# Lower halves of weights subtracted on GpSimd in operations of 128 columns, and later weight blocks cut four steps apart

## The chip, the cores and the metric

The kernel runs on one core of a Trainium2 chip. Its engines work side by side, each through its own queue of instructions: TensorE (PE, with its weight loads as PEld), VectorE (DVE), ScalarE (ACT), GpSimd (POOL) and SyncE (SP), which here issues the DMA transfers. They wait for one another by semaphores. The metric is the device time of one execution in microseconds (us), as the median of several runs.

## The reference

A block with attention and a gated feed-forward part, on x of 2048 rows and 512 columns, in float32:

```
xn  = layernorm(x)                                  # over the 512 columns
q, k, v = split(xn @ wqkv)                          # 32 heads of 16
p   = softmax(mask(q k^T / 4))                      # a row sees itself and the 255 before it
s   = (p v) @ wo
g   = silu( (silu(xn @ w1) * (xn @ w3)) @ w2 )      # 512 -> 1792 -> 512
out = x + s * g
```

## The kernel before

**Numbers.** PE multiplies float16. So that the result has float32 accuracy, every operand is a pair: the upper part `hi` is the value rounded to float16, and the lower part `lo` is what the rounding left, also float16. A product takes three matmuls (hi by hi, lo by hi, hi by lo). A weight must first be brought to the middle of float16's range: the sums of squares of its columns or rows are taken (`squares`, L249 on ACT and L251 on DVE), a tiny matmul spreads them over the partitions, and a chain of DVE operations on one to four columns (`powers`, L294 to L304) makes a power of two of them. Only then can the weight be cut in two.

**Cutting a weight.** A raw weight tile has 128 partitions and 512 columns in float32. `split_pool` cuts it in three steps: ACT multiplies the raw tile by its power of two in place (L342), ACT casts it to float16 (L343), and POOL subtracts the cast from the scaled tile (through `halves`, whose line is L339), in two operations of 256 columns. The 28 tiles of w1 and w3 (two for each of 14 blocks f of the 1792), the ten tiles of w2 with f = 4 to 13 and the four of wo go through it. The first four tiles of w2 and the weights of q, k and v go through `split`, which subtracts on DVE. `halves` serves other work too, above all the cutting of the hidden blocks (`rest` in `gate_up`, behind the cast L1068) and of the attention's output.

**Where PE uses it.** In `gate_up` (matmuls on L1035) PE takes a weight tile in four chunks of 128 columns, for each the upper part, the lower part and the upper part again. In the first quarter of the rows (t = 0) the cut weight is also stored to DRAM, from which the later quarters load it.

**Stages.** The 2048 rows are worked through in four quarters of 512. Attention is made in units (a quarter, a group of eight heads, a half of that), and the feed-forward work is laid between their steps. Weights are measured and cut in the first 175 us or so, during the first quarter, except wo. In the same time the rows of the next quarter are normalised (`rstd`, L464 to L473 on POOL, and `centre`, L476 on DVE), the masks are added (L752, DVE) and the maxima are taken (L678, DVE) and negated (L690 and L691, DVE) and the exponentials taken (L755, ACT). The product of gate and up is finished by L1054 and L1059 on DVE and L1050 on ACT. `measure_down` measures w2: squares on ACT (L922), then small DVE operations (L934 to L944) up to the factor `sw` that scales its tiles on ACT (L342).

**What sets the order.** PE's order is the order in which the program writes its matmuls. It is written in steps: `later(n, f)` puts f in a list to be run n steps on, and `step()`, called after each piece of matmul work, runs what is due. The other engines' orders are made by the tile layer, which places instructions by their dependencies and by when they were written. Tiles lie in 54 buffers (`take`, `give`); `give(..., after=5)` offers a buffer again five steps later, and `take` picks the one that has been free the longest, so that a change of steps also changes which tile lies where.

**Around the change.** `measure(f)` handles two blocks f and f+1, four tiles. Its inner `rest` makes the scales and puts four `cut`s in the list, which the diff touches; `cut` takes a float16 buffer, calls `split_pool` and gives the raw tile back.

Of the kernel before, what the change touches and what calls it, by code (L numbers as in the profile page):

```python
# [21 lines left out]
P = 128  # L22
# [61 lines left out]
def tile_block(ctx: ExitStack, tc: tile.TileContext, x, wqkv, wo, w1, w3, w2, out):  # L84
    nc = tc.nc
# [27 lines left out]
    def take(dtype):  # L113
        free.sort()
        slot = free.pop(0)[2]
        made = fpool.tile([P, 512 if dtype == F32 else 1024], dtype, name=slot, tag=slot, bufs=1)
        held[id(made)] = slot, made
        return made

    def give(*tiles, after=0):  # L120

        for made in tiles:
            given[0] += 1
            free.append((now[0] + after, given[0], held.pop(id(made))[0]))
# [19 lines left out]
    def later(n, f):  # L144
        made_so_far[0] += 1
        queue.append((now[0] + n, made_so_far[0], f))
# [35 lines left out]
    def beside_scores(n, f):  # L182

        later(n, lambda: besides.insert(0, f))
# [55 lines left out]
    def squares(parts, on_act=0, apart=0):  # L240


        ssq = small.tile([P, len(parts)], F32, name="ssq")

        def one(i, raw):

            sq = ppool.tile([P, D], BF16, name="sqa" if i < on_act else "junk", bufs=1)
            if i < on_act:
                nc.scalar.activation(sq, raw, AF.Square, accum_out=ssq[:, i:i + 1])  # L249
            else:  # L250
                nc.vector.tensor_tensor_reduce(out=sq, in0=raw, in1=raw, scale=1.0, scalar=0.0,  # L251
                                               op0=ALU.mult, op1=ALU.add, accum_out=ssq[:, i:i + 1])
        for i, raw in enumerate(parts):
            if apart:
                later(apart * (i + 1), lambda i=i, raw=raw: one(i, raw))
            else:
                one(i, raw)
        sb = small.tile([P, len(parts)], BF16, name="sb")

        def cast():  # L260
            lasts["cast"] = nc.vector.tensor_copy(sb, ssq)
        def behind_bank():

            with tc.issue_after(lasts["emptied"].ins) if "emptied" in lasts else nullcontext():
                cast()
        if apart:
            later(apart * (len(parts) + 1) + 1, behind_bank)
        else:
            cast()
        return sb  # L270

    def powers(sb, n, p2, inv, s=None):


        m = sb.shape[-1] // n
        al = small.tile([P, n], F32, name="al")
        if s is None:
            ps = scores_bank()[:, 0, 0:n]
            for i in range(m):
                nc.tensor.matmul(ps, onesb, sb[:, i * n:(i + 1) * n], start=i == 0, stop=i == m - 1)  # L280
        else:
            for h in range(2):
                for c in range(2):
                    for i in range(m):
                        nc.tensor.matmul(s[64 * c:64 * c + 64, h, WIN:WIN + n],
                                         onesb[64 * h:64 * h + 64, 64 * c:64 * c + 64],
                                         sb[64 * h:64 * h + 64, i * n:(i + 1) * n], start=i == 0, stop=i == m - 1)

        def rest():
            if s is None:  # L290
                nc.vector.tensor_scalar(al, ps, 2.08, 1e-30, op0=ALU.mult, op1=ALU.max)
            else:
                with urgent():
                    nc.vector.tensor_scalar(al, s[:, 0, WIN:WIN + n], 2.08, 1e-30, op0=ALU.mult, op1=ALU.max)  # L294
                    nc.vector.scalar_tensor_tensor(al, s[:, 1, WIN:WIN + n], 2.08, al, op0=ALU.mult, op1=ALU.add)

        def chain():
            nc.vector.tensor_scalar(al.bitcast(I32), al.bitcast(I32), 24, 23, op0=ALU.logical_shift_right,
                                    op1=ALU.logical_shift_left)
            if inv is not None:  # L300

                lasts["scale"] = nc.vector.tensor_scalar(inv.bitcast(I32), al.bitcast(I32), -1.0,
                                                         (2 * 127 - 63 + WS_EXP) * 2.0**23, op0=ALU.mult, op1=ALU.add)
            nc.vector.tensor_scalar(p2, al, 2.0**63, None, op0=ALU.mult)  # L304
        return rest, chain

    def then(s, read, *made):

        first, *rest = *(read if isinstance(read, tuple) else (read,)), *made

        def chain():
            for f in rest:
                f()

        def behind_bank():
            with tc.issue_after(lasts["emptied"].ins) if "emptied" in lasts else nullcontext():
                chain()

        def now_and_later():
            first()  # L320
            later(2, behind_bank)
        if s is not None:
            return now_and_later
        first()
        chain()
# [10 lines left out]
    def halves(op, out, a, b):  # L336

        for c in (slice(0, 256), slice(256, 512)):
            op(out[:, c], a[:, c], b[:, c])  # L339

    def split_pool(hi, lo, raw, s):
        nc.scalar.activation(raw, raw, AF.Copy, scale=s)  # L342
        nc.scalar.copy(hi, raw)  # L343
        halves(nc.gpsimd.tensor_sub, lo, raw, hi)


    WQ = {}
# [524 lines left out]
    def measure(f, apart=0):  # L872

        raws = [RAW.pop(f + i) for i in range(2)]
        sb = squares([raws[0][0], raws[1][0], raws[0][1], raws[1][1]], on_act=4 if f > 2 else 2, apart=apart)

        def scale(s=None):
            pp = small.tile([P, 2, 2], F32, name="pp")
            pi = small.tile([P, 2, 2], F32, name="pi")
            return then(s, powers(sb, 4, pp.rearrange("p a b -> p (a b)"), pi.rearrange("p a b -> p (a b)"), s),  # L880
                        lambda: rest(pp, pi))

        def rest(pp, pi):
            ff = slice(f, f + 2)
            nc.vector.tensor_scalar(sg_scale[:, ff], pp[:, 0, :], 0.5 / (WS * XS), None, op0=ALU.mult)
            nc.vector.tensor_mul(p13[:, ff], pp[:, 0, :], pp[:, 1, :])
            measured.update((f, f + 1))

            def cut(i, k):
                if k == 0:  # L890
                    WF[0, f + i] = [[None, None], WF.pop((0, f + i), [None, None])[1]]
                WF[0, f + i][0][k] = a = take(F16)
                split_pool(a[:, 0:D], a[:, D:], raws[i][k], pi[:, k, i:i + 1])
                give(raws[i][k], after=5)
            for i in range(2):
                for k in range(2):
                    later((1, 2, 4, 6)[2 * i + k], lambda i=i, k=k: cut(i, k))
        if started:
            beside_scores(8, scale)
        else:  # L900
            later(10 if apart else 6, scale)
# [12 lines left out]
    def measure_down(k, f):  # L914
# [17 lines left out]
        def rest(p2):  # L932
            assert measured >= set(range(f0, f1))
            nc.vector.tensor_mul(p2, p2, p13[:, f0:f1])  # L934
            q = small.tile([P, 1], F32, name="q")
            nc.vector.tensor_reduce(q, p2, axis=AX.X, op=ALU.max)
            nc.vector.tensor_scalar(down_scale[:, k:k + 1], q, 1.0 / (HS * WS), None, op0=ALU.mult)
            if k:
                nc.vector.tensor_max(fold_q, fold_q, q)
            else:  # L940
                nc.vector.tensor_copy(fold_q, q)
            nc.vector.reciprocal(q, q)
            sw = small.tile([P, 4], F32, name="sw2")
            nc.vector.tensor_scalar(sw[:, 0:n], p13[:, f0:f1], q, WS, op0=ALU.mult, op1=ALU.mult)  # L944

            def cut(f):
                raw = RAW2.pop(f)
                WF.setdefault((0, f), [[None, None], None])[1] = b = take(F16)
                if k == 0:
                    with tc.issue_after(lasts["emptied"].ins):  # L950
                        split(b[:, 0:D], b[:, D:], raw, sw[:, f - f0:f - f0 + 1])
                else:
                    split_pool(b[:, 0:D], b[:, D:], raw, sw[:, f - f0:f - f0 + 1])
                give(raw, after=5)
            for i, f in enumerate(range(f0, f1)):
                later(1 + 2 * i, lambda f=f: cut(f))
            if f1 == FB:
                later(4, fold_scales)
# [663 lines left out]
    for n, u in enumerate(units):  # L1622
# [17 lines left out]
        k = n // 2 + 2  # L1640
# [35 lines left out]
```

## Time and profile before

| | before |
|---|---|
| median of 3 runs | 813.12 us (813.05 to 813.95) |
| profiled execution | 813.03 us |
| its span | 811.2 us, granted clock 1.000 |
| PE busy | 794.5 us, 98% |
| DVE busy | 634.2 us, 78% |
| ACT busy | 392.5 us, 48% |
| POOL busy | 364.0 us, 45%, 648 instructions |

The span runs from the first to the last instruction of the profiled execution; the rest of its time lies around it. A row of a timeline gives the start and the duration in us, the engine, the line, the operation, output and inputs with shapes, how many instructions the row stands for, and in square brackets how long the engine stood idle before it and what ended that. A row of a group gives the busy time and, behind it, the mean duration of one in ns. A row on a line of the source gives the least, the middle and the greatest duration in ns.

### The profile page before, as it was taken

To read this page: it belongs to the slowest core of one execution; us is meant where nothing else is said; L and a number is where in the kernel's file an instruction comes from. 1 tells how busy PE (TensorE), PEld (TensorE's weight loads), DVE (VectorE), ACT (ScalarE), POOL (GpSimd) and SP (SyncE) were. 2 spreads that over 40 slices of the span, in tenths; PEclk is the share of its full clock that TensorE was granted. 3 is DMA by queue.
4 is the path that set the end of the run, shared out by engine and by line. 5 is a ranking of instruction groups with operands and counts; after the bars stand their busy time and mean duration, and the time that the engine had idled before them with its cause. 6 is when DMAs were issued, how large, how long until landed. Compare 5 with 4: busy or idle time off the path is not lost.

```text
span 811.2 us, 23867 instructions
## 1 busy us (share of the span) xinstructions
PE 794.5 (98%) x9176; PEld 404.2 (50%) x9176; DVE 634.2 (78%) x2037; ACT 392.5 (48%) x591; POOL 364.0 (45%) x648
## 2 busy tenths in 40 slices
PE   8999989999999999999999999999999999999998
PEld 4444444444544444444444454456544654466465
DVE  8788788887898777887988888777777887875437
ACT  6879586563536554445444434344444234344421
POOL 2234266232329546354354355530246277560670
PEclk9999999999999999999999999999999999999999
DMA  9978554835566375657655634656462544335321
GB/s 283 253 221 264 156 190 124 283 117 190 158 180 215 127 249 140 214 145 251 171 162 175 193 98 132 174 150 176 116 189 72 162 138 139 113 85 174 112 67 60
DMA packets 109794, 134.18 MB, mean 165 GB/s; under 512 B 18864, under 2 KB 64880, under 8 KB 109680
## 3 DMA queue, kind: packets, MB, share of 16 engines
q1 hardware_dynamic: 109392, 132.13, 54.7%
q8 instruction: 72, 1.18, 0.6%
q10 hardware_dynamic: 288, 0.52, 0.2%
q14 instruction: 42, 0.34, 0.1%
HBM read 91.23 MB, written 36.57 MB: 158 GB/s over the span
## 4 chain that ended last, share of the span: by engine, by line
PE 80%; DVE 9%; ACT 5%; issue 3%; DMA 2%; SPq 0%; DVEq 0%; POOL 0%; ACTq 0%
PE m L1035 30%; PE po L773 8%; PE m L1260 8%; PE m L1178 8%; PE m L596 7%; PE s L745 5%; PE m L1312 4%; PE m L566 4%; PE s L664 3%; DVE junk L678 2%; PE po L664 2%; ACT sqa L249 1%; ACT slot L342 1%; ACT pt L755 1%; DMA dW<-slot 1%
## 5 line engine op out<-in xcount | busy, mean ns | idle before, releaser
L1035 PE MATMUL m<-XH,slot 128*128 128x512 f16 x896 | 267.3, 380 | 1.6 <-DVE slot L617 1.2
L755 ACT ACTIVATE pt<-s,es 128x1024 f32<-128x1024 f32 x152 | 167.7, 1113 | 192.8 <-DVE s L752 174.6
L339 POOL TENSOR_TENSOR slot<-slot,slot 128x256 f16<-128x256 f32 (+1 forms) x170 | 113.2, 694 | 212.2 <-ACT slot L1068 85.0
L1035 PEld LDWEIGHTS <-slot 128*128 128x128 f16 x1344 | 124.8, 98 | 155.9 <-issue 12.4
L1035 PE MATMUL m<-XL,slot 128*128 128x512 f16 x448 | 169.8, 379 | 0.0
L752 DVE TENSOR_TENSOR s<-s,MK 128x256 f32<-128x256 f32 (+2 forms) x280 | 118.8, 435 | 50.7 <-PE s L745 46.4
L678 DVE CUSTOM_DVE_ANT_0 junk<-s,MW 128x320 bf16<-128x320 f32 x276 | 133.9, 485 | 18.0 <-PE s L664 10.3
L678 DVE CUSTOM_DVE_ANT_0 junk<-po,MW 128x320 bf16<-128x320 f32 x172 | 83.5, 485 | 4.3
L1260 PE MATMUL m<-slot,slot 128*128 128x512 f16 x336 | 78.6, 380 | 0.4 <-DVE slot L1054 0.4
L773 PE MATMUL po<-pt,V 64*32 64x320 f32 (+4 forms) x2880 | 77.2, 342 | 0.8 <-DVE pp L304 0.8
L596 PE MATMUL m<-XH,slot 128*128 128x512 f16 x240 | 70.9, 380 | 1.5 <-DVE slot L1054 0.8
L1178 PE MATMUL m<-slot,slot 128*128 128x256 f16 x588 | 68.4, 273 | 0.0
L1093 POOL TENSOR_TENSOR slot<-slot,slot 128x256 f16<-128x256 f32 x98 | 64.6, 671 | 1.1
L1050 ACT ACTIVATE slot<-m,sgs 128x512 f32<-128x512 f32 x56 | 38.3, 684 | 54.4 <-PE m L1035 53.0
L1178 PEld LDWEIGHTS <-slot 128*128 128x128 f16 x588 | 56.2, 98 | 11.4 <-issue 3.0
L773 PEld LDWEIGHTS po<-pt,V 64*32 64x32 f32 x2880 | 50.4, 106 | 23.0 <-PE s L514 0.9
L1054 DVE SCALAR_TENSOR_TENSOR slot<-slot,m 128x512 f32<-128x512 f32 x56 | 38.3, 684 | 27.9 <-ACT slot L1050 27.8
L745 PE MATMUL s<-qa,KA 50*64 50x320 f16 (+3 forms) x1472 | 58.3, 259 | 0.3 <-DVE M L678 0.2
L596 PEld LDWEIGHTS <-slot 128*128 128x128 f16 x384 | 35.6, 98 | 44.7 <-issue 3.3
L745 PEld LDWEIGHTS <-KA 50*64 50x64 f16 x1472 | 30.1, 105 | 52.1 <-issue 31.4
L1260 PEld LDWEIGHTS <-slot 128*128 128x128 f16 x336 | 30.7, 98 | 38.7 <-issue 4.3
L664 PE MATMUL s<-KA,qa 48*64 48x320 f16 (+3 forms) x824 | 45.0, 294 | 4.1 <-ACT pt L755 2.9
(188 smaller groups left out, 1096.9 us busy)
## 6 DMA issues: line engine op xcount, KB each, us to landing
slot<-dW SPq DMA_DIRECT2D x98, 256.0 KB
slot<-in_B_w_dram SPq DMA_DIRECT2D x56, 256.0 KB
slot<-dFold SPq DMA_DIRECT2D x48, 256.0 KB
dW<-slot SPq DMA_DIRECT2D x42, 256.0 KB
slot<-in_A_x_dram SPq DMA_DIRECT2D x30, 256.0 KB
KA<-dK SPq DMA_DIRECT2D x24, 288.0 KB
qa<-dQ SPq DMA_DIRECT2D x32, 192.0 KB
slot<-dWQ SPq DMA_DIRECT2D x24, 256.0 KB
```

What stands on the lines that cost most here:

```text
L339: op(out[:, c], a[:, c], b[:, c])
L596: nc.tensor.matmul(cell["pp"], w[:, (a * NC + c) * P:(a * NC + c + 1) * P], b[:, c, :], start=(c, i) == parts[0][0], stop=(c, i) == parts[ ...
L664: nc.tensor.matmul(s[c:c + w, r, :n], qa[rows, 2 * p + a, ii * P + c:ii * P + c + w], ka[rows, 2 * p + a, e - n:e], start=True, stop=True)
L678: lasts["maximum"] = nc.vector.tensor_tensor_reduce(out=junk[:, :n], in0=s[:, r, :n], in1=mask, scale=1.0, scalar=NEG, op0=ALU.add, op1=AL ...
L745: nc.tensor.matmul(s[64 * h:64 * h + 64, r, o:o + 64 * n], ka[rows, 2 * p + a, 64 * (m + 4):64 * (m + 5)], qa[rows, 2 * p + a, 64 * (m + k ...
L752: nc.vector.tensor_add(v, v, MK[:, kind, of:of + n, :].unsqueeze(1).to_broadcast([P, 2 * len(which), n, 64]))
L755: lasts["exp"] = nc.scalar.activation(pt, s, AF.Exp, scale=es)
L773: nc.tensor.matmul(cell["po"][32 * i:32 * i + 32, h, 64 * (m + k):64 * (m + k + n)], V[64 * h:64 * h + 64, (4 * t + m // 2) % VB, hd * VW: ...
L1035: nc.tensor.matmul(cell[k], w[:, (a * NC + c) * P:(a * NC + c + 1) * P], b[:, c, :], start=c == 0 and i == 0, stop=c == NC - 1 and i == 2)
L1093: nc.gpsimd.tensor_sub(lo, view, hi)
L1178: nc.tensor.matmul(cell["ps"][:, c], made[:, f:f + P], wj[:, g:g + 256], start=j == j0 and c == 0 and n == 0, stop=j == j1 - 1 and n == 2, ...
L1260: nc.tensor.matmul(ps, hh[:, a * TW + b * P:a * TW + (b + 1) * P], w[:, c * D:(c + 1) * D], start=f == f0 and i == 0, stop=f == f1 - 1 and ...
```

## The change

Two edits.

```
     def split_pool(hi, lo, raw, s):
         nc.scalar.activation(raw, raw, AF.Copy, scale=s)
         nc.scalar.copy(hi, raw)
-        halves(nc.gpsimd.tensor_sub, lo, raw, hi)
+        for c in range(0, 512, P):
+            nc.gpsimd.tensor_sub(lo[:, c:c + P], raw[:, c:c + P], hi[:, c:c + P])
...
             for i in range(2):
                 for k in range(2):
-                    later((1, 2, 4, 6)[2 * i + k], lambda i=i, k=k: cut(i, k))
+                    later(((1, 2, 4, 6) if f < 8 else (1, 5, 9, 13))[2 * i + k], lambda i=i, k=k: cut(i, k))
```

The first edit makes four subtractions of 128 columns out of two of 256, for every tile that `split_pool` cuts; `halves` itself and its other users stay. The second puts the four cuts of the pairs f = 8, 10 and 12 at steps 1, 5, 9 and 13 after their scales are made. The first edit adds a line, so that every line behind L344 has a number one higher in the changed kernel, and the subtraction is L345.

POOL at the place where the pair f = 8 is cut, from about 107 us in the trace; `slot` names are buffers with a number for each use of one. The first row shown is the last of a chain of small operations that normalise the next rows, the rows L339 with `slot_1884` and `slot_2046` (now `slot_1913` and `slot_2085`) are hidden blocks, the first four tiles are of w1 and w3, and the others are of w2. Before:

```order
L473 TENSOR_TENSOR rs<-sq,r_1757 128x4
L339 TENSOR_TENSOR slot_1797<-slot_1076,slot_1797 128x256 x2
L339 TENSOR_TENSOR slot_1811<-slot_1077,slot_1811 128x256 x2
L339 TENSOR_TENSOR slot_1885<-slot_1080,slot_1885 128x256 x2
L339 TENSOR_TENSOR slot_1957<-slot_1081,slot_1957 128x256 x2
L339 TENSOR_TENSOR slot_1884<-slot_1795,slot_1884 128x256 x2
L339 TENSOR_TENSOR slot_1943<-slot_990,slot_1943 128x256 x2
L339 TENSOR_TENSOR slot_1975<-slot_1084,slot_1975 128x256 x2
L339 TENSOR_TENSOR slot_2046<-slot_1973,slot_2046 128x256 x2
L339 TENSOR_TENSOR slot_2034<-slot_1231,slot_2034 128x256 x2
```

and now:

```order
L474 TENSOR_TENSOR rs<-sq,r_1789 128x4
L345 TENSOR_TENSOR slot_1829<-slot_1096,slot_1829 128x128 x4
L345 TENSOR_TENSOR slot_1961<-slot_1097,slot_1961 128x128 x4
L345 TENSOR_TENSOR slot_2064<-slot_1100,slot_2064 128x128 x4
L345 TENSOR_TENSOR slot_2176<-slot_1101,slot_2176 128x128 x4
L339 TENSOR_TENSOR slot_1913<-slot_1827,slot_1913 128x256 x2
L345 TENSOR_TENSOR slot_1974<-slot_1006,slot_1974 128x128 x4
L345 TENSOR_TENSOR slot_2003<-slot_1104,slot_2003 128x128 x4
L339 TENSOR_TENSOR slot_2085<-slot_2001,slot_2085 128x256 x2
L345 TENSOR_TENSOR slot_2071<-slot_1255,slot_2071 128x128 x4
```

Each weight tile has four operations of 128 columns instead of two of 256; the hidden blocks keep their two, and the order of the tiles is the same.

ACT at the same place, from the first scale of f = 8 to the first exponential behind the cuts. Before:

```order
L342 ACTIVATE slot_1076<-slot_1076,pi 128x512
L342 ACTIVATE slot_1077<-slot_1077,pi 128x512
L343 CAST slot_1797<-slot_1076 128x512
L343 CAST slot_1811<-slot_1077 128x512
L342 ACTIVATE slot_1080<-slot_1080,pi 128x512
L342 ACTIVATE slot_1081<-slot_1081,pi 128x512
L343 CAST slot_1885<-slot_1080 128x512
L343 CAST slot_1957<-slot_1081 128x512
L249 ACTIVATE sqa,ssq<-slot_1539 128x512
L1068 CAST slot_1884<-slot_1795 128x512
L755 ACTIVATE pt<-s,es_402 128x1024
```

and now:

```order
L342 ACTIVATE slot_1096<-slot_1096,pi 128x512
L342 ACTIVATE slot_1097<-slot_1097,pi 128x512
L343 CAST slot_1829<-slot_1096 128x512
L343 CAST slot_1961<-slot_1097 128x512
L249 ACTIVATE sqa,ssq<-slot_1567 128x512
L342 ACTIVATE slot_1100<-slot_1100,pi 128x512
L342 ACTIVATE slot_1101<-slot_1101,pi 128x512
L343 CAST slot_2064<-slot_1100 128x512
L343 CAST slot_2176<-slot_1101 128x512
L1069 CAST slot_1913<-slot_1827 128x512
L756 ACTIVATE pt<-s,es_402 128x1024
```

The square L249 of one tile of a later block, which stood behind all four tiles, stands between the second and the third; the rest is in its place.

ACT again, where the pair f = 12 is cut (about 163 to 171 us). Before:

```order
L342 ACTIVATE slot_2051<-slot_2051,pi 128x512
L342 ACTIVATE slot_2052<-slot_2052,pi 128x512
L613 ACTIVATE slot_2842<-m_2822 128x512
L343 CAST slot_2817<-slot_2051 128x512
L343 CAST slot_2829<-slot_2052 128x512
L922 ACTIVATE sqa,ssq_2684<-slot_2651 128x512
L342 ACTIVATE slot_2055<-slot_2055,pi 128x512
L755 ACTIVATE pt<-s,es_719 128x1024
L1050 ACTIVATE slot_2909<-m_2847,sgs 128x512
```

and now:

```order
L342 ACTIVATE slot_2090<-slot_2090,pi 128x512
L923 ACTIVATE sqa,ssq_2742<-slot_2707 128x512
L614 ACTIVATE slot_2901<-m_2886 128x512
L343 CAST slot_2879<-slot_2090 128x512
L342 ACTIVATE slot_2091<-slot_2091,pi 128x512
L342 ACTIVATE slot_2094<-slot_2094,pi 128x512
L343 CAST slot_2957<-slot_2091 128x512
L756 ACTIVATE pt<-s,es_727 128x1024
L1051 ACTIVATE slot_2970<-m_2906,sgs 128x512
```

A square of w2 (L922, now L923) stands ahead of the cast L613 (now L614), and the second and third scales are one place later each. The exponentials L755 (now L756) have as many instructions ahead of them as before. At f = 10 ACT's order is unchanged, and the orders of PE, DVE and SP are the same throughout, but for buffers.

5 lines of the change are left out of this document (3 added, 2 removed).

## The prediction

> **What bounds the kernel now.** I read the page first (busy shares, the chain that ended last), then the stages, then what PE waited for.
>
> ```profile
> PE 794.5 (98%) x9176; PEld 404.2 (50%) x9176; DVE 634.2 (78%) x2037; ACT 392.5 (48%) x591; POOL 364.0 (45%) x648
> ...
> PE 80%; DVE 9%; ACT 5%; issue 3%; DMA 2%; SPq 0%; DVEq 0%; POOL 0%; ACTq 0%
> ```
>
> PE is busy for 794.5 of 811.2 us. POOL, the engine that the change loads, is idle for more than half the span and is no part of the chain. The stages (columns: us; then busy of PE, PEld, DVE, ACT, POOL; clock; DMA):
>
> ```profile
> 0.00:30.00 30.00, 27.54 (x129) 12.71 (x129) 23.64 (x75) 21.93 (x42) 5.33 (x33) 1.00 0.96 267
> 30.00:80.00 50.00, 46.89 (x348) 20.52 (x348) 43.21 (x174) 42.40 (x89) 23.38 (x34) 1.00 0.82 248
> 80.00:135.00 55.00, 49.84 (x613) 24.44 (x611) 45.45 (x171) 38.96 (x73) 23.91 (x44) 1.00 0.54 164
> 135.00:175.00 40.00, 38.62 (x427) 18.50 (x426) 32.87 (x120) 25.05 (x42) 18.86 (x31) 1.00 0.61 201
> 175.00:811.00 636.00, 631.55 (x7664) 328.01 (x7662) 488.99 (x1501) 264.15 (x349) 292.52 (x507) 1.00 0.51 152
> ```
>
> From 175 us on PE idles 4.5 us in 636, so nothing done to another engine there is worth much, and what is won or lost before 175 us carries through to the end. Before it PE idles 2.5, 3.1, 5.2 and 1.4 us. Nearly all the weights are cut there (w1, w3 and w2), so the change is decided there, above all between 80 and 135 us.
>
> ```profile
> PE s L664 <- ACT pt L755: 2.9, 3, 1.6
> ...
> PE m L596 <- DVE slot L1054: 0.8, 1, 0.8
> ...
> PEld L1035 <- POOL slot L339: 1.3, 1, 1.3
> ```
>
> PE waits for ACT and DVE. No wait of PE itself names POOL; once a weight load, which runs ahead of its matmul, did. So POOL matters only by what it does to DVE and ACT.
>
> **The split into 128 columns: its price.** 28 tiles of w1/w3, 10 of w2 (f = 4 to 13) and 4 of wo go through `split_pool`: 42 tiles, 84 operations become 168. No row shows a subtraction of 128 columns, so I bound it.
>
> ```profile
> L339 POOL TENSOR_TENSOR slot<-slot,slot 128x256 f16<-128x256 f32 x140 | 92.0, 686 | 150.5 <-ACT slot L1068 85.0 <-ACT slot L343 65.1
> L1093 POOL TENSOR_TENSOR slot<-slot,slot 128x256 f16<-128x256 f32 x98 | 64.6, 671 | 1.1
> ...
> L464 POOL TENSOR_TENSOR sq<-r 128x4 f32<-128x4 f32 x3 | 0.6, 201 | 11.8 <-DVE r L447 11.8
> ...
> masks.py:199 POOL TENSOR_SCALAR_AFFINE_SELECT identh<-identh 128x128 f16<-128x128 f16 x1 | 0.3, 293 | 0.0
> ```
>
> 256 columns take 671 ns undisturbed, 4 columns 201. The straight line gives 201 + 124 × (671 − 201)/252 = 432 ns for 128. Below it lies the half of 671, 336 (no fixed part; the one-input select of 128 columns, 293, is under even that); above it 671, no saving. I take 432: both its points are the same operation. The four of the run at 117.90, quoted next, take 2.56 us, so they follow each other every (2.56 − 0.67)/3 = 0.63 us, 0.04 less than one lasts; the new spacing is then about 0.39 us (0.30 to 0.63), and a tile takes 1.56 instead of 1.26 us. Over 42 tiles that is +12.6 us of POOL (0 to +53), beside 447 idle us.
>
> The Trainium skill (GPSIMD Engine Reference, 3.1) gives about 2.6 cycles per element for two inputs and 4497 ns at 2048 elements; at 1.2 GHz this leaves 60 ns fixed, an estimate of 337 ns for 128 columns and 5 us over the 84 added operations. The 201 ns of four columns speak against so small a fixed part. The same page (7, Performance pitfalls) warns of many small reads, some 102 cycles each that do not overlap; that speaks against this change, and no run here shows it by itself.
>
> Does the first weight come late? Its two operations open this run:
>
> ```profile
> 32.74 5.97 POOL L339 TENSOR_TENSOR slot<-slot,slot 128x256 f16<-128x256 f32 x8 [26.85 <-ACT slot L343]
> 107.47 6.69 POOL L339 TENSOR_TENSOR slot<-slot,slot 128x256 f16<-128x256 f32 x10
> 117.90 2.56 POOL L339 TENSOR_TENSOR slot<-slot,slot 128x256 f16<-128x256 f32 x4 [3.74 <-ACT slot L343]
> ...
> 36.88 0.59 PE L1035 MATMUL m<-XH,slot 128*128 128x512 f16 x2
> ```
>
> They end by about 34.1 and PE begins with that weight at 36.88, nearly 3 us of cover against +0.3 for one tile. Later tiles have more. PE's loads now wait for each quarter instead of each half; what is already there makes no wait. Cost: 0 (at no saving, one tile is 1.3 us late, still covered).
>
> **What POOL does to DVE.** This I did not look for and found in DVE's rows of the long run, 107.47 to 114.16:
>
> ```profile
> 107.55 0.87 DVE L476 TENSOR_SCALAR slot<-slot,mv,rs 128x512 f32<-128x512 f32 x1 [0.38 <-POOL rs L473]
> ...
> 108.41 0.82 DVE L476 TENSOR_SCALAR slot<-slot,mv,rs 128x512 f32<-128x512 f32 x1
> ...
> 111.00 0.68 DVE L690 TENSOR_SCALAR NM<-M 128x16 f16<-128x16 f32 x1
> ...
> 111.93 0.38 DVE L691 SCALAR_TENSOR_TENSOR NM<-M,NM 128x16 f16<-128x16 f32 x1
> ...
> 112.85 0.71 DVE L298 TENSOR_SCALAR al<-al 128x4 int32<-128x4 int32 x1
> 113.47 0.97 DVE L476 TENSOR_SCALAR slot<-slot,mv,rs 128x512 f32<-128x512 f32 x1
> 114.36 0.15 DVE L304 TENSOR_SCALAR pp<-al 128x4 f32<-128x4 f32 x1
> 114.44 0.53 DVE L476 TENSOR_SCALAR slot<-slot,mv,rs 128x512 f32<-128x512 f32 x1
> ...
> 115.72 0.23 DVE L944 TENSOR_SCALAR sw<-p,q 128x4 f32<-128x4 f32 x1
> 115.86 0.68 DVE L1054 SCALAR_TENSOR_TENSOR slot<-slot,m 128x512 f32<-128x512 f32 x1
> ...
> L690 DVE TENSOR_SCALAR NM<-M x32: 164/192/697, 45.2 to 736.5; 128x16 f16<-128x16 f32 x32
> ...
> L691 DVE SCALAR_TENSOR_TENSOR NM<-M,NM x32: 159/210/741, 45.4 to 736.7; 128x16 f16<-128x16 f32 x32
> L298 DVE TENSOR_SCALAR al<-al x17: 135/159/712, 9.3 to 242.3; 128x4 int32<-128x4 int32 x9, 128x1 int32<-128x1 int32 x6, 128x3 int32<-128x3 int32 x2
> ```
>
> L476 takes 0.53 us once POOL is still (114.44), and 0.87, 0.82, 0.97 beside it; L690 at best 164 ns and here 680; L298 at best 135 and here 710 (159 in the middle). They lie on SBUF alone, and end some 0.03 us after a POOL operation has: the DVE operation waits until POOL's current one is over. Against 0.53 us for L476, 0.17 for L690 and L691 and 0.16 for L298 the six lose 0.34 + 0.29 + 0.51 + 0.21 + 0.55 + 0.44 = 2.34 us. DVE has no gap in this stretch, and what stands behind it is waited for:
>
> ```profile
> 113.99 0.25 PE L664 MATMUL s<-KA,qa 48*64 48x128 f16 x4 [0.60 <-ACT pt L755]
> ...
> 116.59 0.59 PE L596 MATMUL m<-XH,slot 128*128 128x512 f16 x2 [0.81 <-DVE slot L1054]
> ...
> 120.02 0.30 PE L664 MATMUL s<-KA,qa 48*64 48x256 f16 x4 [1.62 <-ACT pt L755]
> ...
> 115.98 1.33 ACT L342 ACTIVATE slot<-slot,sw 128x512 f32<-128x512 f32 x2 [0.86 <-DVE sw L944]
> ...
> 37.43 0.68 DVE L261 CAST sb<-ssq 128x2 bf16<-128x2 f32 x1 [0.33 <-ACT sqa L249]
> ...
> 162.87 0.71 DVE L298 TENSOR_SCALAR al<-al 128x4 int32<-128x4 int32 x1
> ...
> L339 POOL TENSOR_TENSOR slot<-slot,slot x170: 662/672/1119, 32.7 to 754.8; 128x256 f16<-128x256 f32 x140, 128x256 f32<-128x256 f32 x30
> ```
>
> ACT waits for L944, then works without a gap up to the exponential L755 for which PE waits 1.62 us; PE waits 0.81 for L1054 itself.
>
> So a shorter POOL operation lets DVE in sooner, but the run lasts longer. Stepping through the stretch by hand with a boundary every 0.39 us: the four tiles (16 operations from 107.47) end near 113.7 where undisturbed, 114.4 with the lengthening that DVE causes (the run of ten took 6.69 for 6.3), against 112.9 before. L690, L691 and L298 lose 0.2 to 0.3 each and the third L476 begins near 112.3, 1.2 us earlier. But the two operations that cut the hidden block behind the tiles stay at 256 columns, and now run from 114.4 to 115.7, where they hold up L304, the fourth L476, L934, L939 and L944, which run free now. L944 ends near 115.75 against 115.95: −0.2 us. A spacing of 0.36 gives −0.7, one of 0.42 gives +0.25, so about 15 us of time per us of spacing. The ends: −2.3 if all stalls went, and at no saving (0.63) eleven such operations × 0.45 − 2.34 = +2.6.
>
> The run at 32.74 holds up DVE likewise (its cast L261 lasts 0.68 at 37.43), but shorter stalls are paid for by a run that grows by 8 × 0.15 = 1.2 us into the small operations behind it: ±0.2, 0 taken. At 161 to 163 us the same L690, L691 and L298 meet a run (0.71 at 162.87, again 0.55 lost); of this I take a third back, −0.2. After 175 us PE has no gap for any of it.
>
> **The later cuts.** For f = 8, 10 and 12 the cuts are due at steps 1, 5, 9, 13 instead of 1, 2, 4, 6. PE, DVE, SP and POOL keep their order. On ACT one square (L249) passes two scales and two casts of f = 9, and four places near 163 us swap; the tiles that the cuts free and take are other slots. ACT has gaps of 0.55 and 1.08 us behind the first place:
>
> ```profile
> 111.12 0.62 ACT L1068 CAST slot<-slot 128x512 f16<-128x512 f32 x1 [0.55 <-DVE slot L1059]
> 112.82 1.11 ACT L755 ACTIVATE pt<-s,es 128x1024 f32<-128x1024 f32 x1 [1.08 <-DVE s L752]
> ```
>
> A square and its read-out move 0.8 us, the gaps hold 1.6. Cost 0; without that cover, +0.8. The f = 9 tiles reach POOL 0.8 us later, while it still works off f = 8. Other slots change which store or load waits for which tile; the load and store queue has its order, and I take 0 (−0.3 to +0.5, the gaps of PE in that stage).
>
> **Sum.** PE 0, POOL +12.6 hidden, stretch at 107 −0.2, others −0.2, cuts 0: −0.4. The profiled execution took 813.03 us (811.2 of span and 1.8 around it), 0.1 under the median of 813.12. 812.6 on it, 812.7 against the median.
>
> **Rivals.** 0.2%, 1.63 us, is about what a measurement tells from no change; 811.5 and 814.75 are the bounds.
>
> 1. *No fixed part.* At 336 ns the spacing is about 0.30; the tiles end at 112.9 as before, the block behind them at 114.2, and the small operations after 114.36 stay free while the stalls ahead fall from 2.34 to about 1.1. −1.2 there, −0.2 elsewhere: 811.7. For it: the select at 293. Against: 201 ns for four columns. By the 337 ns worked out from the Trainium skill (GPSIMD Engine Reference, 3.1) this would be the outcome.
> 2. *More than the stretch.* The earlier end also closes PE's waits of 0.60, 0.81 and 1.62, to which ACT adds its own gap: at most 3.0 us if all vanish, and in the middle between this and rival 1's 1.4, −2.2: 810.9. For it: these waits are all behind DVE. Against: ACT's queue is full from 116 on and moves only by L944's gain.
> 3. *The fixed part is larger: slower.* If an operation of 128 columns lasts 0.55 us (spacing 0.51), the line of 15 us per us gives 0.12 × 15 − 0.2 = +1.6 in the stretch at 107; with the others +1.8: 814.9. That spacing is the point from which it is slower by over 0.2%; from 0.41 on it is a loss at all. For it: a POOL operation beside DVE lasts up to 1.12 instead of 0.67 us, and twice as many may be lengthened twice as often. Against: both ends of the line are measured.
> 4. *The cuts do not do as said.* The steps hardly move an instruction, so the second edit is worth 0; that is in the sum.
>
> **How the numbers follow.** Forecast, with rival 4 in it (−1.0 to +0.6, so 812.1 to 813.7 its own range) 0.42; rival 1 0.20, a third of it past −1.63; rival 2 0.14; rival 3 0.24, five sixths of it past +1.63. Faster 0.07 + 0.14 = 0.21; slower 0.20; within 0.59. The range reaches to rivals 2 and 3 and leaves out their far ends: 811.0 to 814.8.
>
> **What would show it.** In the changed profile: subtractions 128x128 at 0.40 to 0.46 us; L690 (now at 111.00) and the L298 after it under 0.5 us; the 128x256 pair behind the four tiles after 114 us with L934 or L944 lengthened beside it; PE's busy time unchanged, no wait of PE for POOL. A subtraction over 0.5 us or a PE wait that names POOL makes the prediction wrong upward; one under 0.36 us, or PE's gaps from 113.99 to 120.02 closed, downward.

## The result, and the profile after

The changed kernel takes 811.37 us in the median of 13 runs (811.12 to 811.56) against 813.12 (812.91 to 814.04) for the kernel before, run beside it: ratio 0.9977, 95% interval 0.9969 to 0.9984, so it is faster by 1.75 us. Its profiled execution took 811.24 us, the span 809.4, at clock 1.000.

The page of the changed kernel, the busy times and the chain that ended last:

```profile
PE 793.7 (98%) x9176; PEld 403.7 (50%) x9176; DVE 631.2 (78%) x2037; ACT 392.1 (48%) x591; POOL 377.1 (47%) x732
...
PE 79%; DVE 8%; ACT 6%; DMA 3%; issue 2%; SPq 1%; POOL 0%; ACTq 0%; DVEq 0%
```

POOL is busy for 13.1 us more, and its share of the chain is still 0%. DVE is busy for 3.0 us less, though it does the same work: its operations last less long. The stages of the changed kernel, without the first:

```profile
30.00:80.00 50.00, 47.45 (x350) 20.75 (x351) 41.53 (x176) 43.03 (x89) 27.80 (x58) 1.00 0.82 245
...
80.00:135.00 55.00, 50.53 (x643) 24.98 (x642) 45.72 (x173) 39.90 (x74) 29.25 (x73) 1.00 0.53 164
...
135.00:175.00 40.00, 38.81 (x402) 18.39 (x401) 33.03 (x126) 24.76 (x42) 21.75 (x50) 1.00 0.62 204
...
175.00:809.00 634.00, 629.78 (x7656) 327.02 (x7654) 487.25 (x1492) 262.53 (x347) 293.03 (x519) 1.00 0.51 152
```

PE's idle time falls from 3.1 to 2.6 us (30 to 80 us), from 5.2 to 4.5 (80 to 135) and from 1.4 to 1.2 (135 to 175). From 175 us on it is 4.2 in place of 4.5. The groups on POOL:

```profile
L345 POOL TENSOR_TENSOR slot<-slot,slot 128x128 f16<-128x128 f32 x168 | 69.1, 446 | 58.3 <-ACT slot L343 58.3
...
L339 POOL TENSOR_TENSOR slot<-slot,slot 128x256 f16<-128x256 f32 x56 | 36.6, 674 | 76.8 <-ACT slot L1069 76.7
```

An operation of 128 columns lasts 446 ns in the mean. In the stretch that the prediction was about, POOL's two rows are

```profile
106.77 6.98 POOL L345 TENSOR_TENSOR slot<-slot,slot 128x128 f16<-128x128 f32 x16
...
113.71 1.29 POOL L339 TENSOR_TENSOR slot<-slot,slot 128x256 f16<-128x256 f32 x2
```

16 operations in 6.98 us, and the hidden block at 113.71. On DVE, in the same stretch of the changed kernel:

```profile
106.85 0.63 DVE L477 TENSOR_SCALAR slot<-slot,mv,rs 128x512 f32<-128x512 f32 x1 [0.37 <-POOL rs L474]
...
107.47 0.57 DVE L477 TENSOR_SCALAR slot<-slot,mv,rs 128x512 f32<-128x512 f32 x1
...
109.82 0.17 DVE L691 TENSOR_SCALAR NM<-M 128x16 f16<-128x16 f32 x1
...
110.22 0.17 DVE L692 SCALAR_TENSOR_TENSOR NM<-M,NM 128x16 f16<-128x16 f32 x1
...
110.92 0.17 DVE L298 TENSOR_SCALAR al<-al 128x4 int32<-128x4 int32 x1
...
111.01 0.73 DVE L477 TENSOR_SCALAR slot<-slot,mv,rs 128x512 f32<-128x512 f32 x1
...
111.66 0.39 DVE L304 TENSOR_SCALAR pp<-al 128x4 f32<-128x4 f32 x1
...
111.97 0.73 DVE L477 TENSOR_SCALAR slot<-slot,mv,rs 128x512 f32<-128x512 f32 x1
...
112.62 0.38 DVE L935 TENSOR_TENSOR pp<-pp,p 128x4 f32<-128x4 f32 x1
...
113.68 0.72 DVE L945 TENSOR_SCALAR sw<-p,q 128x4 f32<-128x4 f32 x1
...
114.32 0.68 DVE L1055 SCALAR_TENSOR_TENSOR slot<-slot,m 128x512 f32<-128x512 f32 x1
```

L477 (L476 before) loses 0.10, 0.04, 0.20 and 0.20 us against 0.53; L691, L692 and L298 lose nothing; L304 and L935 lose 0.24 and 0.23 against 0.15; L945 loses 0.49 against the 0.23 that it took before, to the first half of the hidden block. That is 1.50 us in place of 2.34: 0.84 us less. In three other profiles (the changed kernel again, the first edit alone, and 128 columns for the pair f = 8 alone) the same ten operations lose some 1.45 us, differently shared out: L691 loses 0.30 or 0.31 there, and L945 only 0.11. What one operation is spared, another pays.

PE's instructions stand in the same order in both traces, so the start of each can be set against its start before. Changed minus before, in us, at some of PE's instructions (times in the trace of before):

```
at     8.84  +0.05     before any weight is cut
at    30.67  -0.52     PE waits for qa, a transfer
at    42.60  -0.32
at    74.41  -0.72
at   100.13  -0.69     ahead of the stretch
at   113.99  -1.92
at   116.59  -1.54     behind it
at   166.50  -1.86
the last     -1.78
```

The stretch from 100 to 117 us gives 0.85 us of the 1.78, the time between 43 and 74 us 0.40, and the place at 166 us 0.32. The first 0.32 comes from a wait for a transfer at 30 us, ahead of POOL's first subtraction. In a second profile of the changed kernel (one of the experiments below) PE stands at −0.06 at 42.60, so this start belongs to the execution and not to the change; but there too it stands at −0.72 at 74.41, where it waits for DVE (L1054 before, L1055 now). So the stretch from 43 to 74 us gives 0.40 in one profile and 0.66 in the other; the other two places give 0.89 and 0.31 in the second profile.

PE's waits behind the stretch, in the changed kernel:

```profile
112.07 0.25 PE L665 MATMUL s<-KA,qa 48*64 48x128 f16 x4
...
115.04 0.59 PE L597 MATMUL m<-XH,slot 128*128 128x512 f16 x2 [1.19 <-DVE slot L1055]
...
118.47 0.30 PE L665 MATMUL s<-KA,qa 48*64 48x256 f16 x4 [1.62 <-ACT pt L756]
```

The wait of 0.60 us for the exponential, which stood at 113.99, is gone, and the one for L1055 (L1054 before) is 1.19 instead of 0.81: PE came 1.92 us early to it, DVE 1.54. The wait of 1.62 for the next exponential is what it was.

### The profile page after: what moved, and what is told of

The parts are those of the page before. It is cut to its first block, busy times and chain, and to the rows that moved or that the text cites. A ratio compares the mean times of both kernels' runs of the same rounds, so it can differ in the third digit from the quotient of the medians.

```text
span 809.4 us, 23944 instructions
## 1 busy us (share of the span) xinstructions
PE 793.7 (98%) x9176; PEld 403.7 (50%) x9176; DVE 631.2 (78%) x2037; ACT 392.1 (48%) x591; POOL 377.1 (47%) x732
## 3 DMA queue, kind: packets, MB, share of 16 engines
q8 instruction: 72, 1.18, 0.6%
## 4 chain that ended last, share of the span: by engine, by line
PE 79%; DVE 8%; ACT 6%; DMA 3%; issue 2%; SPq 1%; POOL 0%; ACTq 0%; DVEq 0%
PE m L1036 30%; PE po L774 8%; PE m L1261 8%; PE m L1179 8%; PE m L597 7%; PE s L746 5%; PE m L1313 4%; PE m L567 4%; PE s L665 3%; DMA slot<-in_B_w_dram 2%; DVE junk L679 2%; PE po L665 2%; ACT slot L342 1%; ACT pt L756 1%; ACT sqa L249 1%
## 5 line engine op out<-in xcount | busy, mean ns | idle before, releaser
L756 ACT ACTIVATE pt<-s,es 128x1024 f32<-128x1024 f32 x152 | 167.5, 1112 | 193.7 <-DVE s L753 186.5
L339 POOL TENSOR_TENSOR slot<-slot,slot 128x256 f16<-128x256 f32 (+1 forms) x86 | 57.7, 692 | 141.9 <-ACT slot L1069 76.7
L345 POOL TENSOR_TENSOR slot<-slot,slot 128x128 f16<-128x128 f32 x168 | 69.1, 446 | 58.3 <-ACT slot L343 58.3
L1055 DVE SCALAR_TENSOR_TENSOR slot<-slot,m 128x512 f32<-128x512 f32 x56 | 38.3, 684 | 29.0 <-ACT slot L1051 29.0
```

The source lines that it names most:

```text
L345: nc.gpsimd.tensor_sub(lo[:, c:c + P], raw[:, c:c + P], hi[:, c:c + P])
L756: lasts["exp"] = nc.scalar.activation(pt, s, AF.Exp, scale=es)
```

## The experiments

Theory A: DVE's operations that work on SBUF alone wait for POOL's operation in progress, so shorter operations cost DVE less. Theory B: the later cuts, with other buffers and times of loads, bring the gain. Theory C: the runs of POOL are at a length where more operations cost what shorter ones win.

**One edit at a time.** The first edit alone:

```
 def split_pool(hi, lo, raw, s):
...
-    halves(nc.gpsimd.tensor_sub, lo, raw, hi)
+    for c in range(0, 512, P):
+        nc.gpsimd.tensor_sub(lo[:, c:c + P], raw[:, c:c + P], hi[:, c:c + P])
```

> The first edit alone: 128 columns per subtraction, all cuts due at steps 1, 2, 4, 6 as before. Theory A (the time lies in DVE's waits for POOL's current operation): nearly the whole gain stays, 811.3 to 811.9 against 813.1 of before, and the six DVE operations between 107 and 114 us lose under 0.8 us together, as in the changed kernel. Theory B (the later cuts, with other buffers and other times of loads, bring it): 812.8 to 813.4.

811.61 us (811.21 to 819.92) against 813.07; ratio 0.9989, interval 0.9973 to 1.0005, made wide by one run at 819.92, so that it holds 1, no change; the other eleven runs all lie under the lowest of the kernel before (812.75). In its trace the stretch from 100 to 117 us gives 0.89 us, as in the changed kernel. The second edit alone (cuts of f = 8, 10 and 12 at steps 1, 5, 9, 13, subtractions of 256 columns):

> The second edit alone: two subtractions of 256 columns, cuts of f = 8, 10, 12 at steps 1, 5, 9, 13. Theory A: 812.7 to 813.3, the stalls between 107 and 114 us still 2.0 to 2.5 us; at most 0.2 us comes from the square that ACT takes ahead of the second scale near 163 us. Theory B: 811.2 to 811.8.

813.15 us (812.88 to 814.46), ratio 0.9999, interval 0.9990 to 1.0008. The six operations lose 0.34 + 0.29 + 0.51 + 0.21 + 0.55 + 0.44 us there, as in the kernel before. Theory B falls: the second edit alone gives nothing that its runs can tell, and the first alone gives 1.46 of the 1.75 us by the medians. In the traces the second edit has a small share at one place: between 120 and 166.50 us PE wins 0.13 us with it alone, 0.19 with the first alone and 0.31 with both.

**One place alone.** 128 columns only for the four tiles of the pair f = 8:

```
-    def split_pool(hi, lo, raw, s):
+    def split_pool(hi, lo, raw, s, w=256):
...
-        halves(nc.gpsimd.tensor_sub, lo, raw, hi)
+        for c in range(0, 512, w):
+            nc.gpsimd.tensor_sub(lo[:, c:c + w], raw[:, c:c + w], hi[:, c:c + w])
...
-                split_pool(a[:, 0:D], a[:, D:], raws[i][k], pi[:, k, i:i + 1])
+                split_pool(a[:, 0:D], a[:, D:], raws[i][k], pi[:, k, i:i + 1], P if f == 8 else 256)
```

> 128 columns only in the four tiles of the pair f = 8, everything else as before. Theory A with the stretch at 107 us as the main place: 0.8 us of the gain, 812.3. If the gain is spread over all the runs of POOL: 812.8 to 813.0. If the stretch gives back what it wins further on: 813.1.

812.21 us (811.81 to 814.02) against 813.07, ratio 0.9990, interval 0.9981 to 0.9999. In its trace PE stands +0.04 us against before at 8.84, −0.21 at 108.54, −0.88 at 113.99 and −0.86 at the last instruction. Four of 42 tiles give half of the gain, at the place that the prediction named, and nothing is given back behind it.

**The other side of the size.** One subtraction of 512 columns per tile:

> The kernel before with one subtraction of 512 columns per weight tile. By the line through 4 and 256 columns it lasts 1.15 us. Theory A: each DVE operation that meets it waits up to 1.1 us, so the six stalls between 107 and 114 us grow from 2.3 to some 4 us: 814 to 816, slower. If only the number of POOL instructions or their total time counted: 812 to 813, since POOL is 2 us less busy.

814.49 us (814.1 to 816.1) against 813.13, ratio 1.0019, interval 1.0010 to 1.0028: slower by 1.36 us, with POOL less busy. The run of the pair f = 8 and the first two L476 in its trace, then a place at 67 us:

```profile
108.29 4.87 POOL L344 TENSOR_TENSOR slot<-slot,slot 128x512 f16<-128x512 f32 x4
...
108.37 1.35 DVE L476 TENSOR_SCALAR slot<-slot,mv,rs 128x512 f32<-128x512 f32 x1 [0.38 <-POOL rs L473]
...
109.72 1.31 DVE L476 TENSOR_SCALAR slot<-slot,mv,rs 128x512 f32<-128x512 f32 x1
...
67.21 1.07 DVE L944 TENSOR_SCALAR sw<-p,q 128x4 f32<-128x4 f32 x1
...
68.92 0.59 PE L1035 MATMUL m<-XH,slot 128*128 128x512 f16 x2 [0.84 <-DVE slot L1054]
```

Four operations in 4.87 us, 1.19 each in the mean over all 42 (1.15 by the line), and L476 at 1.35 and 1.31 instead of 0.53. The time came out as expected, but not at the place that was expected. In the stretch behind 107 us the six operations lose 2.26 us and not some 4: the first two L476 lose 1.60 of it, and L691 and L298, at 113.44 and 114.14, find POOL between two operations or at the end of one and lose nothing. PE stands at +0.83 us against before at 100.13 and at +0.75 at 116.59, so this stretch costs nothing. The loss lies at other meetings of the same kind: +1.07 us between 30 and 74 us, as at 67.21, where L944 takes 1.07 us instead of 0.23 and PE waits 0.84 for L1054 behind it, and +0.49 at 164 us. Eight subtractions of 64 columns:

> The kernel before with eight subtractions of 64 columns per weight tile. By the same line one lasts 0.31 us and a tile takes 2.2 us instead of 1.3. Theory A with its price: the stalls get shorter but the runs of POOL 70% longer, and the hidden block behind them comes 3 us later: 811.4 to 813, no better than 128 columns. If only the length of one operation counts: 810.5 to 811.

813.64 us (812.66 to 817.98), ratio 1.0009, interval 0.9997 to 1.0020: the gain is gone, and the time lies above the 813 that theory A allowed. An operation of 64 columns lasts 0.32 us and follows the one before after 0.265. In the stretch at 107 us it did more than 128 columns: PE goes from +0.99 us at 108.54 to −0.19 at 116.59, 1.18 won, where the changed kernel wins 0.60 between the same points. But in the run that cuts the first weights (POOL, DVE and PE rows of this kernel, and the durations of L334):

```profile
32.77 10.41 POOL L345 TENSOR_TENSOR slot<-slot,slot 128x64 f16<-128x64 f32 x32 [26.88 <-ACT slot L343]
...
40.20 2.55 DVE L334 SCALAR_TENSOR_TENSOR slot<-slot,sw,slot 128x512 f16<-128x512 f32 x2 [0.19 <-ACT slot L333]
...
43.40 0.59 PE L1036 MATMUL m<-XH,slot 128*128 128x512 f16 x2 [0.61 <-DVE slot L1055]
...
L334 DVE SCALAR_TENSOR_TENSOR slot<-slot,sw,slot x12: 745/790/1905, 11.4 to 75.5; 128x512 f16<-128x512 f32 x12
```

POOL is at work from 32.77 for 10.41 us; L334, two operations that take 1.42 us when POOL is still, take 2.55, and PE waits 0.61 us for L1055 behind them. In the kernel before, POOL's run has ended at 38.71, ahead of L334 at 40.54. The longer run is one part of the account. Another is that the first L334, at 40.20, takes 1.84 us instead of 0.75: it waits through four whole operations of 64 columns and not for the one in progress, and so does the one of 1.905 at 69.73 us; a cast L261 at 120.42 waits through three. Places of this kind between 30 and 76 us lose 1.3 us. So there is a best size: 512 columns 814.5, 256 columns 813.1, 128 columns 811.6, 64 columns 813.6 by the medians. So theory C is right from 128 to 64 columns, and not from 256 to 128.

**What the stretch can give at most.** The lower halves of the pair f = 8 set to zero by a POOL operation that reads nothing, in place of the subtractions; for the other tiles `halves` stays:

```
-    halves(nc.gpsimd.tensor_sub, lo, raw, hi)
+    nc.gpsimd.memset(lo, 0.0)
```

> The kernel before, but the lower halves of the four tiles of the pair f = 8 are set to zero by one POOL operation each that reads nothing, so the subtraction is left out there. What the stretch at 107 us can give at most. Theory A: all of the 2.3 us of stalls goes, or all but what the first zeroing costs: 810.8 to 811.6. If PE's own waits there are set by ACT and not by DVE: 812 to 812.5, no more than the 128 columns gave for this pair (812.2).

812.03 us (811.71 to 821.09), ratio 1.0003 with an interval of 0.9980 to 1.0026 that two far runs (818.69 and 821.09) make useless; its medians differ by 1.10 us, little more than with 128 columns for this pair. In its trace PE goes from −0.01 us at 42.60 to −1.68 at 116.59, and ends at −1.16; the 0.5 us given back come at 328 us and later and are not explained. So by this one trace the stretch can give some 1.7 us, of which 128 columns take half. The same for all 42 tiles:

> The same for all 42 weight tiles: no subtraction of weights on POOL, lower halves zero. What the meetings of DVE with the cutting of weights cost altogether. Theory A: below the changed kernel by what is left of its stalls, 809.5 to 811. If the changed kernel has already won nearly all: 811 to 811.5.

813.56 us (812.89 to 814.88), ratio 1.0007, interval 0.9999 to 1.0016: no gain, against both expectations. It was not the clean removal that it was meant to be. A zeroing does not wait for ACT's cast, so it stands elsewhere in POOL's queue, and it holds DVE up too:

```profile
108.72 1.45 POOL L344 MEMSET slot<- 128x512 f16 x3
...
108.83 1.63 DVE L476 TENSOR_SCALAR slot<-slot,mv,rs 128x512 f32<-128x512 f32 x1 [0.63 <-POOL rs L473]
```

L476 waits here for all three zeroings, 1.1 us. This run says nothing on what the subtractions cost altogether.

**A version that goes further.** The changed kernel, with the hidden blocks of the first two quarters cut in 128 columns too:

```
-    halves(nc.gpsimd.tensor_sub, hh[:, TW:], sg, hh[:, 0:TW])
+    for c in range(0, TW, P):
+        nc.gpsimd.tensor_sub(hh[:, TW + c:TW + c + P], sg[:, c:c + P], hh[:, c:c + P])
```

> The changed kernel, with the hidden blocks' subtraction (behind the cast of the hidden block, first two quarters of the rows) in operations of 128 columns too. Theory A: in the changed kernel the factor sw waits 0.5 us for an operation of 256 columns at 113.7 us, and two operations of the power's chain lose 1.0 us near 162; with 128 columns about half of that goes: 810.9, range 810.6 to 811.4. Rival C (the runs of POOL are at the length where more operations cost what shorter ones win): 811.3 to 812.

810.93 us (810.58 to 811.18), ratio 0.9970, interval 0.9958 to 0.9982: the fastest kernel of the study, 2.1 us under the kernel before. That it is faster than the changed kernel is likely and not shown: the intervals overlap. Its rows behind the stretch:

```profile
113.66 0.48 DVE L945 TENSOR_SCALAR sw<-p,q 128x4 f32<-128x4 f32 x1
...
114.79 0.59 PE L597 MATMUL m<-XH,slot 128*128 128x512 f16 x2 [0.94 <-DVE slot L1055]
```

L945 takes 0.48 instead of 0.72, and PE waits 0.94 instead of 1.19 for L1055. At 166 us PE stands at −2.53 us against before, where the changed kernel has −1.86; this profile loses 0.6 of it again at 530 us, as that of the second edit alone loses 0.55 there, in a stage that none of the edits touches. The same kernel without the later cuts, and the changed kernel again beside it:

> Weights and hidden blocks in operations of 128 columns, but all cuts due at steps 1, 2, 4, 6: the best kernel so far (810.93) without the second edit. If the later cuts are worth nothing beside shorter operations: 810.8 to 811.1. If they win by where the square stands on ACT and by how the boundaries of POOL's operations fall (0.3 us of stall of L690 in the first edit alone that the changed kernel does not have, and 0.2 near 166 us): 811.2 to 811.5.

> The changed kernel once more, beside the two others on one chip: 811.1 to 811.6.

811.24 us (811.0 to 811.75; ratio 0.9974, interval 0.9964 to 0.9984) and 811.28 (811.09 to 812.64; 0.9975, 0.9966 to 0.9984), against 813.24. By the medians the later cuts are worth 0.3 us beside shorter operations (810.93 and 811.24), which is less than these runs can tell. Beside each other on one chip, the kernel with shorter hidden blocks but without the later cuts (811.24) and the changed kernel (811.28) are the same. The second profile of the changed kernel also takes one reason away: L691, which loses 0.30 us in the first edit alone and nothing in the changed kernel's first profile, has this row in the second:

```profile
109.83 0.48 DVE L691 TENSOR_SCALAR NM<-M 128x16 f16<-128x16 f32 x1
```

It loses 0.31 us here, in the same kernel, so the later cuts do not decide whether it is held up. In both profiles it starts 0.02 us ahead of one of POOL's operations.

**64 columns where they helped.** The fastest kernel with 64 columns in the pair f = 8 alone:

> The best kernel so far, with 64 columns in the pair f = 8 alone. With 64 columns everywhere the stretch at 107 us gained 1.2 us and the time was lost in runs before it. Theory A: 0.3 us more than with 128 columns, 810.6. If the longer run of POOL holds up the hidden block and w2 behind it: 811.0 to 811.5.

815.87 us (815.32 to 816.72), ratio 1.0032, interval 1.0021 to 1.0043: slower by 2.6 us than before (813.24), against both expectations. In its trace the stretch itself is as good as hoped (PE waits 0.45 us for L1055), and the loss comes a few us later. Rows of POOL (L1071 cuts the hidden blocks in this kernel), the durations of L261 (least, middle, greatest, in ns), then one row of DVE and one of ACT:

```profile
106.88 9.36 POOL L345 TENSOR_TENSOR slot<-slot,slot 128x64 f16<-128x64 f32 x32
...
116.20 1.58 POOL L1071 TENSOR_TENSOR slot<-slot,slot 128x128 f16<-128x128 f32 x4
...
117.74 3.13 POOL L345 TENSOR_TENSOR slot<-slot,slot 128x128 f16<-128x128 f32 x8
...
120.83 1.58 POOL L1071 TENSOR_TENSOR slot<-slot,slot 128x128 f16<-128x128 f32 x4
...
122.37 1.58 POOL L345 TENSOR_TENSOR slot<-slot,slot 128x128 f16<-128x128 f32 x4
...
L261 DVE CAST sb<-ssq x13: 158/170/5422, 8.6 to 242.1; 128x4 bf16<-128x4 f32 x9, 128x2 bf16<-128x2 f32 x4
...
118.56 5.42 DVE L261 CAST sb<-ssq 128x4 bf16<-128x4 f32 x1 [1.61 <-ACT sqa L249]
...
124.74 1.11 ACT L756 ACTIVATE pt<-s,es 128x1024 f32<-128x1024 f32 x1 [4.58 <-DVE s L753]
```

The longer run of the pair leaves POOL no pause until 123.95. A cast of four columns on DVE (L261, 0.17 us in the middle) starts in the middle of that and is not let in at any boundary: it waits through thirteen whole operations, 5.4 us, until POOL runs dry. Everything on DVE stands behind it, and ACT's exponential waits 4.58 us. Was it the row of equal operations that shut DVE out?

> The changed kernel with 64 columns in the pair f = 8, hidden blocks at 256 as in the changed kernel: the 64 columns without the shorter hidden blocks, with which a cast on DVE (L261) waited 5.4 us for fourteen POOL operations of 128 columns in a row and the kernel took 815.9. POOL's run behind the pair then starts 0.3 us earlier, which is no whole number of operations of 0.386 us. If any back-to-back run of short POOL operations shuts DVE out until it ends: the cast waits 2 us or more, 813 to 815. If DVE is let in or passed over by where its request falls within POOL's operation: one operation's wait, 811.0 to 811.6.

816.19 us (814.71 to 817.11), ratio 1.0034, interval 1.0023 to 1.0045: the long wait of the first expectation, with a higher price. POOL and DVE of this kernel, then three stretches (us; PE, PEld, DVE, ACT, POOL; clock; DMA), and last one stretch of the kernel above (815.87):

```profile
116.25 1.30 POOL L339 TENSOR_TENSOR slot<-slot,slot 128x256 f16<-128x256 f32 x2
...
117.50 3.13 POOL L345 TENSOR_TENSOR slot<-slot,slot 128x128 f16<-128x128 f32 x8
...
120.58 1.30 POOL L339 TENSOR_TENSOR slot<-slot,slot 128x256 f16<-128x256 f32 x2
...
121.84 1.58 POOL L345 TENSOR_TENSOR slot<-slot,slot 128x128 f16<-128x128 f32 x4
...
118.61 4.84 DVE L261 CAST sb<-ssq 128x4 bf16<-128x4 f32 x1 [1.61 <-ACT sqa L249]
...
122.00:124.50 2.50, 0.91 (x5) 0.30 (x3) 2.43 (x6) 0.29 (x1) 1.42 (x4) 1.00 0.00 0
...
124.50:128.00 3.50, 0.75 (x18) 0.40 (x17) 3.17 (x12) 3.50 (x8) 0.39 (x2) 0.75 0.02 6
...
128.00:132.00 4.00, 3.86 (x28) 1.79 (x29) 3.53 (x14) 2.56 (x6) 1.20 (x4) 0.50 0.70 228
...
118.00:122.00 4.00, 4.00 (x48) 1.87 (x48) 3.44 (x1) 2.16 (x5) 4.00 (x12) 0.62 0.04 12
```

The cast waits again until the run ends, 4.8 us, past operations of both lengths and with its start elsewhere within POOL's operation (0.34 us after its beginning, 0.04 in the kernel above). So neither the equal pieces nor the place of the request explains it. Leaving the zeroings aside, DVE waits through more than one whole operation of POOL only in the three kernels that have operations of 64 columns: here, in the kernel above, and at the three places with 64 columns for all tiles. In each case the request falls into a run of POOL without a pause. But the run at 107 us in the kernel before had no pause either, and there DVE was let in; and with 64 columns for all tiles two more L334 (72.51 and 75.52 us) meet runs of that kind and wait through one operation at most. So the condition stays open.

The wait has a sequel in this kernel: PE, busy for 1.66 of the 6 us from 122 to 128, has a granted clock of 0.75 in the second part of them and of 0.50 in the next 4 us. In the kernel above the clock is 0.62 already from 118 to 122 us, with PE busy all the time and DVE's wait still going on, so the two profiles do not show one cause for the lower clock.

## Why the prediction was right or wrong

The measured 811.37 lies in the range, on the side that was forecast, 1.3 us under the forecast of 812.7; the result crosses the bound of 0.2% by a tenth of a us, while "within" had most of the chance. The sum itself, −0.4, is less than a quarter of what was measured, and its own range (812.1 to 813.7) does not hold the result: the wider range does, because it was drawn out towards rival 2. That part is luck; the mechanism and the place are not.

- **The price of an operation** was right: 446 ns in the mean against 432, a spacing of 6.98 / 16 = 0.44 us beside DVE and 0.385 between two that DVE does not touch, against 0.39; POOL +13.1 us against +12.6. It was hidden, as said: PE has no wait for POOL. The 337 ns estimated from the Trainium skill (GPSIMD Engine Reference, 3.1) is 0.11 us too low here.
- **Where it is decided** was right: DVE's waits for POOL's operation in progress, and the stretch at 107 us. That the same four tiles alone give 0.86 us shows it for half of the gain; for the other half the traces give the places, and no run changes those alone. One reading in it is too wide: L690, L691 and L298 end 0.03 us after a POOL operation, but the three L476 end 0.28 after one. The Trainium skill (SBUF — State Buffer, "Who interferes with whom") has GpSimd and some of DVE's operations share a pair of ports that one of them holds for a whole instruction; L476 at 0.53, 0.87 and 1.35 us beside nothing, 256 and 512 columns agrees with that.
- **The term that was mis-sized** is the stretch: −0.2 forecast, −0.85 measured. The step that failed is the one through DVE's operations by hand. POOL's side of it came out: the pair of the hidden block began 6.94 us behind the start of the run (113.71 − 106.77), forecast 6.9. But L690, L691 and L298 were to lose 0.2 to 0.3 us each, and lost 0.01 together in one profile and some 0.34 together in three others; the third L476 began 4.24 us behind the start and not 4.8. So DVE was far enough ahead that of the five small operations which the pair was to hold up only L945 met it (0.49 us); L304, the fourth L476 and L935 had met operations of 128 columns, at 0.2 each, and L940 none.
- **"Others −0.2"** was too small as well: −0.40 between 43 and 74 us (−0.66 in the second profile), where the prediction took 0, and −0.32 at 166, where it took −0.2.
- **The later cuts at 0** were right as far as the runs can tell: 813.15 against 813.07 alone. Their 0.13 us at 166 us stand in the traces only.
- **Rival 1** gave a number, 811.7, nearer the result than the forecast, with a spacing of 0.30 that is not what was measured. Its other half did not happen either: the small operations behind the tiles were not free but lost 1.16 us, and the six ahead lost 0.34 and not 1.1. That its −1.2 for the stretch comes nearer than the forecast is luck. **Rival 2** failed: of PE's three waits the one of 0.60 us went, the one of 1.62 is unchanged and the one for L1055 grew. **Rival 3**'s size did not occur at 128 columns; the mechanism behind it, longer runs that hold DVE up, is what the 64 columns showed, by other prices than its line of 15 us per us. Rival 3's sum also adds 0.2 for the other places, where the forecast takes 0.2 off, and gives no reason; with the forecast's sign it would be 814.5.

## What to carry to other kernels

An engine that is idle half the time can still set the pace by how long one of its operations holds what another engine needs: read the durations of the other engine's small operations beside it (least, middle, greatest), not its waits, for these stalls stand in no list of waits. Cut such work into pieces only as far as the run of pieces still ends before the other engine's next work: here 128 columns won 1.5 us by the medians and 64 lost it again. The lowest median (810.93) came with the neighbour in the same queue cut as well, which is not shown to be better. A hand step through one stretch gives the sign and the place; which operation is held up depends on boundaries a few hundredths of a us apart, while the sum of the stalls hardly changed from profile to profile (1.45 to 1.50 us in four).

## What the runs showed of the hardware that was not expected

- DVE is not always let in at the next boundary. In most places it waited for the POOL operation in progress, or for the next where that began within a few hundredths of a us of it. In an unbroken run of POOL a cast of four columns waited for thirteen (5.42 us) and eleven (4.84 us) whole operations, in two kernels, and every run of these took over 814.7 us; with 64 columns for all tiles, two L334 waited through four (1.84 and 1.905 us instead of 0.75) and a cast through three. All of these are in kernels with operations of 64 columns. What decides is open; pieces of one length and of two, and two places of the request within POOL's operation, gave the same.
- A POOL operation that only writes (a zeroing of 512 columns, 0.52 us) holds up L476 too: 1.63 us instead of 0.53 beside three of them, of which it waited for all.
- The long wait on DVE was followed by a lower granted clock: 0.50 for 4 us in one kernel, in which PE fell back from +2.44 us against before to +4.30 and then made up a part (+3.25 at 166 us). How much of the 4.9 us between this kernel and the changed one (816.19 and 811.28) is the clock is not measured apart; in the other kernel the clock was 0.62 during the wait.
